# The last transform of a long convolution in eight 64x32 tiles, and the order of its gates, copies and stores

## The chip, the cores and the metric

The kernel runs on one core of one Trainium2 chip. Its engines work side by side, each on its own queue in order: TensorE (PE in the profile; PEld is its weight load), VectorE (DVE), ScalarE (ACT), GpSimd (POOL) and SyncE (SP), which here only issues DMAs. ACT and POOL can issue DMAs too. The metric is the device time of one execution in microseconds, as the median of several runs.

## The reference

A block in the manner of S4 with a gated feed-forward part, in float32, for L = 2048 positions and D = 512 channels:

```
xn = layernorm(x)
s  = causal_conv(xn, K) + xn * Dskip      # K from A, B, C, log_dt; done by FFTs of length 2L
g  = silu(gelu(xn @ w1 + b1) @ w2 + b2)
out = x + s * g
```

The convolution has one kernel of 2048 taps for each channel.

## The kernel before

A first long part (to about 400 us) makes the convolution kernels and the feed-forward part, whose gates g lie in DRAM in `gd`. The change does not touch it. The second part does the convolution for four blocks b of 128 channels. A transform over 2048 positions is split into N1 = 32 by N2 = 64, and for each block these steps run:

- `first_dft` (L873): matmuls over the 32, for the input and for the convolution kernel; ACT copies the result to SBUF (`X`, L879).
- `second_dft` (L892): matmuls over the 64, in 64x64 tiles. ACT copies the spectrum of the input (`uh`, L900), DVE multiplies it with that of the kernel (`product`, L909) and forms sums and differences (`combine`, L919 and L921, into `Y`).
- `back_dft` (L927, `sa`): the transform back over the 64; ACT copies into `Z` (L936).
- `swing` (L942, `w`): 128x128 transposes of `Z`, two for each of four row blocks q4; ACT, or DVE for some copies of the last block, copies to `bs` (L950).
- `last_dft` (L969, `y`): the transform back over the 32, with the cosine table `gc`. For one q4 it is two matmuls (jj = 0, 1) of 128 rows and 64 columns, 512 wide, into the two halves of one PSUM bank. Half of the table's entries are zeros: each of its 128 rows belongs to one of two interleaved halves hh of the output rows.
- `last_out`: DVE multiplies by the gate (L974, `gb`), POOL adds x (L975, `xb`); `store` (L981) writes the result, and `tail_load` (L959, L961) has fetched gate and x.

The order of the work is written out by hand. `slot(b, g)` for g = 0 to 7 does the second transforms of four of the 32 frequencies of block b, and beside them, in even slots, a quarter of the first transform of block b+1, in odd slots the back transform of a quarter that is done, and the last steps (swings, last transform, gate, store) of block b-1: in blocks 1 and 2 the swings stand in slots 3 and 5, two q4 each, and the last transforms in slots 5 and 7, two q4 each; in block 3 one q4 per slot, swings in slots 3 to 6 and last transforms in 4 to 7. Within a slot the instructions go out in the order second, first, back, copies, product, combine, last transform and gate and store, swings, loads. Block 3's own last steps run after its slot 7.

PSUM banks for all but the second transform come from `bank` (L821), in turn from two pools of two buffers. A matmul into a bank waits until the copy or the gate that read its last content is done. A tile of SBUF that is used again waits in the same way: the gate and x tiles of blocks 0 to 2 have three buffers each. All loads and stores of the last steps are issued by SP, in program order; for block 3 they go to a tile (`big`, called `last`) in a buffer that the transforms no longer need.

Of the kernel before, what the change touches and what calls it, by code (L numbers as in the profile page):

```python
# [125 lines left out]
def _shape_constants():  # L126
# [40 lines left out]
def kernel(  # L167
# [5 lines left out]
    V, A, GP, PE, SY = nc.vector, nc.scalar, nc.gpsimd, nc.tensor, nc.sync  # L173

    x_l = u[0].rearrange("(r j q) d -> j r q d", j=2, q=NQ)
    o_l = out[0].rearrange("(r j q) d -> j r q d", j=2, q=NQ)

# [627 lines left out]
    def open_mid():  # L805
        SB["pm"] = pm = opened(p2, "pm", "right")
        SB["ps"] = opened(pz, "psm", "left", bufs=2, space=PSUM)
        SB["tcn"] = pm.tile([P, N1, P], F32, name="tcn")
        SB["gc"] = pm.tile([P, 2 * N1], F32, name="gc")

# [118 lines left out]

    def back_out(b, j, h, eng=A):  # L930
        if (b, "Z") not in yy:
            yy[b, "Z"] = SB["pm"].tile([P, 4, 8, N1, 4], F32, tag="Z", name=f"Z{b}", bufs=2)
        k = 8 * j + 4 * h
        src = yy.pop((b, j, h)).rearrange("p k (x h) -> p x k h", h=4)
        dst = yy[b, "Z"].rearrange("p r q k h -> p (r q) k h")[:, :, k:k + 4, :]
        eng.copy(dst, src) if eng is A else eng.tensor_copy(dst, src)  # L936

    def swing(b, q4, jj):
        Z = yy[b, "Z"].rearrange("p (j r) (t q) k h -> p j r t q (k h)", j=2, t=2)
        p = bank(f"w{b}_{q4}_{jj}")  # L940
        for e in range(4):
            PE.transpose(p[:, e, :], Z[:, jj, q4 // 2, q4 % 2, e, :], ident)  # L942
        yy[b, q4, jj] = p

    def swing_out(b, q4, jj):
        if jj == 0:
            yy[b, q4, "s"] = SB["pm"].tile([P, 2, 4, P], F32, tag="bs", name=f"bs{b}_{q4}", bufs=3)
        dst = yy[b, q4, "s"][:, jj].rearrange("p e (x r) -> p e r x", r=2)
        src = yy.pop((b, q4, jj)).rearrange("p e (r x) -> p e r x", r=2)
        A.copy(dst, src) if jj or b < NB - 1 else V.tensor_copy(dst, src)  # L950

    gx = {}

    def tail_load(b, q4):
        cs = slice(b * P, (b + 1) * P)
        n = slice(4 * q4, 4 * q4 + 4)
        t = gx.pop((b, q4, "t"), None) or new_tail(b, q4)
        gx[b, q4] = t
        SY.dma_start(t[0], gd[b].rearrange("p (q m) -> p q m", m=P)[:, n])  # L959
        for j in range(2):  # L960
            SY.dma_start(t[1][j * 64:(j + 1) * 64], x_l[j, :, n, cs])  # L961

    def new_tail(b, q4):
        return tuple(SB["pm"].tile([P, 4, P], F32, tag=m, name=f"{m}{b}_{q4}", bufs=3) for m in ("gb", "xb"))

    def last_dft(b, q4):
        py = bank(f"y{b}_{q4}")
        for jj in range(2):
            PE.matmul(py[64 * jj:64 * jj + 64], SB["gc"], yy[b, q4, "s"][:, jj], start=True, stop=True, skip_group_check=True)  # L969
        gx[b, q4, "y"] = py  # L970

    def last_out(b, q4, eng):
        gb, xb = gx[b, q4]
        V.tensor_mul(gb, gx.pop((b, q4, "y")), gb)  # L974
        eng.tensor_add(xb, gb, xb)  # L975

    def store(b, q4):
        cs = slice(b * P, (b + 1) * P)
        xb = gx.pop((b, q4))[1]
        for j in range(2):  # L980
            SY.dma_start(o_l[j, :, 4 * q4:4 * q4 + 4, cs], xb[j * 64:(j + 1) * 64])  # L981

# [4 lines left out]

    def lasts(b, q4, eng=GP):
        last_dft(b, q4)
        last_out(b, q4, eng)  # L990

    def slot(b, g):
# [60 lines left out]
    with tc.manual_schedule():  # L1053
# [79 lines left out]
```

## Time and profile before

| | us |
|---|---|
| median of three runs | 598.95 |
| lowest, highest | 595.91, 600.62 |
| the profiled execution | 600.56 |
| its span, first to last instruction | 598.80 |

All times in the text are counted from the start of the span. PE is granted 0.98 of its full clock in the mean. The rows of the profile stand in the prediction. A row of a timeline is start, duration of the merged stretch, engine, line, operation, output <- inputs, shape, count, and in brackets the idle time ahead and what ended it. Each float32 matmul shows as two records. Durations of neighbouring matmuls overlap by the pipeline's depth; the distance from one start to the next tells what a group costs.

### The profile page before, as it was taken

Reading aid. Unit: us, or ns where it says so; the run is one execution under the profiler, and the core shown is the slowest. Engines: PE = TensorE matmul, PEld = TensorE weight load, DVE = VectorE, ACT = ScalarE, POOL = GpSimd, SP = SyncE. Lnnn points to the kernel's source line nnn. Section 1 sums busy time; section 2 is a strip of 40 time slices with the busy share of each in tenths; the row PEclk is TensorE's granted clock in tenths of the full one; section 3 lists DMA queues with packets and bytes.
Section 4 is the critical chain, followed back from the end, with each engine's and each line's share of the span. In section 5 each row is a group of like instructions: output and inputs, shape, how many; then the busy total and the mean of one; then the engine's idle time right before and its main releaser. Section 6 shows DMA issues by size and latency. Waiting matters only on the chain.

```text
span 598.8 us, 16788 instructions
## 1 busy us (share of the span) xinstructions
PE 551.5 (92%) x7064; PEld 440.8 (74%) x7064; DVE 466.2 (78%) x745; ACT 423.2 (71%) x613; POOL 267.8 (45%) x362
## 2 busy tenths in 40 slices
PE   1968999999959999999998999989999999999995
PEld 1656777777737777777776777767889887887872
DVE  5999998899999979999968898960047645765884
ACT  2567878699876999997999898853355555464442
POOL 1545646844577666597364656820220204202121
PEclk9989999999989999999999999989999999999998
DMA  8984522194717284205624338049846593613957
GB/s 189 322 232 132 198 63 91 40 297 134 252 54 281 86 272 146 99 22 175 178 75 165 92 119 104 23 124 297 225 151 75 148 104 71 177 40 74 186 123 152
DMA packets 100288, 86.62 MB, mean 145 GB/s; under 512 B 43538, under 2 KB 88850, under 8 KB 97140
## 3 DMA queue, kind: packets, MB, share of 16 engines
q1 hardware_dynamic: 97584, 67.71, 44.4%
q0 software_dynamic: 2624, 17.83, 8.3%
q8 instruction: 55, 0.90, 0.6%
q14 instruction: 21, 0.17, 0.1%
q10 hardware_dynamic: 4, 0.00, 0.0%
HBM read 51.97 MB, written 33.55 MB: 143 GB/s over the span
## 4 chain that ended last, share of the span: by engine, by line
PE 51%; DVE 7%; ACT 6%; DMA 3%; issue 2%; POOL 0%; DVEq 0%; ACTq 0%; POOLq 0%
PE s L892 10%; PE s L873 7%; PE sa L927 5%; PE f L245 4%; PE z L292 4%; PE f L246 4%; PE f L247 4%; PE z L293 3%; PE z L294 3%; PE kg L643 3%; PE w L942 2%; PE y L969 2%; DVE e L628 1%; PE ph L582 1%; DVE e L632 1%
## 5 line engine op out<-in xcount | busy, mean ns | idle before, releaser
L605 POOL TENSOR_TENSOR mm<-mm,rc 128x32 f32<-128x32 f32 (+4 forms) x150 | 104.7, 698 | 11.8
L292 PE MATMUL z<-w2h,hh 128*128 128x512 f32 x224 | 96.0, 429 | 0.2 <-ACT hh L270 0.2
L245 PE MATMUL f<-xh,w1h 128*128 128x512 f32 x220 | 93.4, 424 | 0.5 <-ACT hf L264 0.5
L294 PE MATMUL z<-w2h,hl 128*128 128x512 f32 x224 | 88.0, 393 | 0.4 <-DVE hl L280 0.4
L293 PE MATMUL z<-w2l,hh 128*128 128x512 f32 x224 | 87.7, 392 | 0.0
L246 PE MATMUL f<-xl,w1h 128*128 128x512 f32 x220 | 86.8, 395 | 0.0
L247 PE MATMUL f<-xh,w1l 128*128 128x512 f32 x220 | 86.3, 392 | 0.0
L909 DVE TENSOR_TENSOR t<-s,uh 128x512 f32<-128x512 f32 x64 | 41.2, 686 | 47.0 <-ACT uh L900 46.8
L280 DVE TENSOR_TENSOR hl<-hf,hh 128x512 fp32r<-128x512 f32 x56 | 42.4, 764 | 31.4 <-ACT hh L270 31.3
L892 PE MATMUL s<-X,mc 64*64 64x128 f32 x2048 | 63.1, 272 | 0.0
L892 PEld LDWEIGHTS s<-X,mc 64*64 64x64 f32 x2048 | 55.8, 133 | 5.1 <-issue 3.3
L602 POOL COPY mm<-rc 128x32 f32<-128x32 f32 x30 | 12.6, 420 | 102.8 <-DVE e L635 94.7
L628 DVE TENSOR_TENSOR e<-mm,ra 128x1024 f32<-128x1024 f32 x32 | 45.9, 1433 | 15.0 <-ACT ra L616 12.5
L879 ACT COPY X<-s 128x512 f32<-128x512 f32 x64 | 33.2, 598 | 32.6 <-PE s L873 32.6
L975 POOL TENSOR_TENSOR xb<-gb,xb 128x512 f32<-128x512 f32 x12 | 15.1, 1274 | 85.9 <-DVE gb L974 73.4
L245 PEld LDWEIGHTS f<-xh,w1h 128*128 128x128 f32 x220 | 42.4, 193 | 11.7 <-ACT hf L264 2.7
L294 PEld LDWEIGHTS z<-w2h,hl 128*128 128x128 f32 x224 | 42.2, 188 | 11.1 <-DVE hl L280 1.9
L264 ACT ACTIVATE hf<-f,b1s 128x512 f32<-128x512 f32 x56 | 38.2, 687 | 16.3 <-PE f L247 13.7
L292 PEld LDWEIGHTS z<-w2h,hh 128*128 128x128 f32 x224 | 42.5, 190 | 9.5 <-issue 0.7
L247 PEld LDWEIGHTS f<-xh,w1l 128*128 128x128 f32 x220 | 41.9, 190 | 9.1
L246 PEld LDWEIGHTS f<-xl,w1h 128*128 128x128 f32 x220 | 42.0, 191 | 8.1 <-DVE xl L380 0.2
L293 PEld LDWEIGHTS z<-w2l,hh 128*128 128x128 f32 x224 | 42.4, 189 | 7.4
(153 smaller groups left out, 1208.7 us busy)
## 6 DMA issues: line engine op xcount, KB each, us to landing
x<-in_A_u_dram SPq DMA_DIRECT2D x16, 256.0 KB
xs<-x SPq DMA_DIRECT2D x16, 256.0 KB
xt_h<-xh POOLq DMA_DIRECT2D x4, 1024.0 KB, 5.3
xt_l<-xl POOLq DMA_DIRECT2D x4, 1024.0 KB, 8.6
kgd<-ko SPq DMA_DIRECT2D x32, 128.0 KB
za<-zo SPq DMA_DIRECT2D x4, 1024.0 KB
xh<-xt_h POOLq DMA_DIRECT2D x4, 1024.0 KB, 5.8
xl<-xt_l POOLq DMA_DIRECT2D x4, 1024.0 KB, 7.9
```

Of the source, the lines that this page charges most:

```text
L245: PE.matmul(p, wh[:, k, :], xh[:, k, :], start=(k == 0), stop=False)
L246: PE.matmul(p, wh[:, k, :], xl[:, k, :], start=False, stop=False)
L247: PE.matmul(p, wl[:, k, :], xh[:, k, :], start=False, stop=(k == KD - 1))
L280: V.tensor_sub(hl, hf, hh)
L292: PE.matmul(z, hh[:, s], wh, start=(f0 == 0 and f > 0), stop=False)
L293: PE.matmul(z, hh[:, s], wl, start=False, stop=False)
L294: PE.matmul(z, hl[:, s], wh, start=False, stop=(f0 == FA - 1))
L605: GP.tensor_mul(mv[:, :, 0:3:2, w:2 * w], mv[:, :, 0:3:2, 0:w], rc[:, 2 + 2 * i:4 + 2 * i, :].rearrange("p j c -> p c j").unsqueeze(3).to_ ...
L628: V.tensor_mul(e1, m1.unsqueeze(1).to_broadcast([P, 2, CH, N1]), ra[:, :, :, :N1])
L873: PE.matmul(p[:, i, :], src[r, 2 * i:2 * i + 2, :], fc[r], start=True, stop=True, skip_group_check=True)
L892: PE.matmul(p[ka * 64:(ka + 1) * 64, r, o, :, jj], mc[h, k, ((0, 2), (1, 0))[c][o], :], xf[b][h, c, :, k, :], start=(c == 0), stop=(c == 1 ...
L909: V.tensor_mul(t, p[:, i, :, 1].unsqueeze(1).to_broadcast([P, 2, 2, P]), uh)
```

## The change

- The table `gc` loses its zeros: 128 rows by 32 columns, with the two halves hh above one another. `last_dft(b, t)` takes two q4 at once (t = 0, 1) and does eight matmuls of 64 rows by 32 columns, 512 wide, into two banks (h = 0, 1), four column groups each. `Z` is laid out anew so that the rows of one half stand together.
- A unit of gate, x and output is now (t, h). Its rows lie differently in DRAM, so that a load takes six DMAs (two for the gate, four for x) where it took three, and a store four where it took two.
- In the slots of blocks 1 and 2 the last transform, its gates and its stores go out straight behind the second transform of slots 5 and 7, ahead of the back transform, the copies and the products. In block 3 the last transform stands there too, in slots 4 and 7, with gates and stores behind the sums; its swings come one slot earlier, in slots 2 to 5.
- Block 2's units 2 and 3 get a buffer of their own (`spare`), and their loads come in slots 2 and 3. Block 3's own loads are issued by POOL in slots 1 to 4, instead of SP in slots 2, 3, 6 and 7.
- At the end, the last copy into Z is halved between ACT and DVE; the copies of q4 = 2 and 3 go to ACT alone; the last transforms come behind the third and the fourth swing; of each pair of gates POOL adds x to the first and DVE to the second; and stores go to SP, ACT and, for the last two, POOL.

```diff
-    cg = np.zeros((2, 2, N1, N1, 2))
-    for hh in range(2):
-        cg[hh, 0, :, :, hh] = np.cos(a).T
-        cg[hh, 1, :, :, hh] = -np.sin(a).T
-    cg = cg.transpose(2, 0, 1, 3, 4).reshape(P, 2 * N1)
+    cg = np.stack([np.cos(a).T, -np.sin(a).T], 1)
+    cg = np.stack([cg, cg]).reshape(P, N1)
...
-    def back_out(b, j, h, eng=A):
+    def back_out(b, j, h, engs=(A,)):
         if (b, "Z") not in yy:
-            yy[b, "Z"] = SB["pm"].tile([P, 4, 8, N1, 4], F32, tag="Z", name=f"Z{b}", bufs=2)
+            yy[b, "Z"] = SB["pm"].tile([P, 32, 2, N1, 2], F32, tag="Z", name=f"Z{b}", bufs=2)
...
-        A.copy(dst, src) if jj or b < NB - 1 else V.tensor_copy(dst, src)
+        A.copy(dst, src) if jj or b < NB - 1 or q4 > 1 else V.tensor_copy(dst, src)
...
+    def tail_load(b, i, q=SY):
...
+        for a in range(2):
+            r = slice(a * 64, (a + 1) * 64)
+            q.dma_start(t[0][r], gd[b].rearrange("(j n h) (t a q m) -> t h a j n q m", n=N1, h=2, t=2, a=2, m=P)[i // 2, i % 2, a])
+            for j in range(2):
+                r = slice(a * 64 + j * N1, a * 64 + (j + 1) * N1)
+                q.dma_start(t[1][r], x_t[i // 2, i % 2, a, j, :, :, cs])
...
-    def last_dft(b, q4):
-        py = bank(f"y{b}_{q4}")
-        for jj in range(2):
-            PE.matmul(py[64 * jj:64 * jj + 64], SB["gc"], yy[b, q4, "s"][:, jj], start=True, stop=True, skip_group_check=True)
-        gx[b, q4, "y"] = py
+    def last_dft(b, t):
+        py = [bank(f"y{b}_{t}_{h}") for h in range(2)]
+        for a in range(2):
+            for jj in range(2):
+                for h in range(2):
+                    r, m = slice(h * 64, (h + 1) * 64), N1 * (2 * a + jj)
+                    PE.matmul(py[h][m:m + N1], SB["gc"][r], yy[b, 2 * t + a, "s"][r, jj], start=True, stop=True, skip_group_check=True)
+        gx[b, t, "y"] = py
+
+    def last_out(b, t, engs):
+        py = gx.pop((b, t, "y"))
+        for h in range(2):
+            gb, xb = gx[b, 2 * t + h]
+            V.tensor_mul(gb, py[h], gb)
+            engs[h].tensor_add(xb, gb, xb)
+
+    def store(b, t, qs=((SY, SY), (SY, SY))):
+        cs = slice(b * P, (b + 1) * P)
+        for h in range(2):
+            xb = gx.pop((b, 2 * t + h))[1]
+            for a in range(2):
+                for j in range(2):
+                    r = slice(a * 64 + j * N1, a * 64 + (j + 1) * N1)
+                    qs[h][a].dma_start(o_t[t, h, a, j, :, :, cs], xb[r])
...
-        sw = {3: (0,), 4: (1,), 5: (2,), 6: (3,)} if last else {3: (0, 1), 5: (2, 3)}
-        ls = {4: (0,), 5: (1,), 6: (2,), 7: (3,)} if last else {5: (0, 1), 7: (2, 3)}
+        sw = {2: (0,), 3: (1,), 4: (2,), 5: (3,)} if last else {3: (0, 1), 5: (2, 3)}
+        ls = {4: (0,), 7: (1,)} if last else {5: (0,), 7: (1,)}
         second_dft(b, g)
+        if b:
+            for q4 in ls.get(g, ()):
+                last_dft(b - 1, q4)
+                if not last:
+                    last_out(b - 1, q4, (GP, GP))
+                    store(b - 1, q4)
...
-        if b:
-            for q4 in ls.get(g, ()):
-                lasts(b - 1, q4)
-                store(b - 1, q4)
+        if last:
+            for q4 in ls.get(g, ()):
+                last_out(b - 1, q4, (GP, GP))
+                store(b - 1, q4)
...
-        if b and g in (0, 1, 2, 5):
-            tail_load(b - 1, (0, 1, 2, 5).index(g))
-        if last and g in (2, 3, 6, 7):
-            tail_load(b, (2, 3, 6, 7).index(g))
+        if last and g == 2:
+            spare = SB["pf"].tile([P, 4, 4, P], F32, tag="in", name="spare", bufs=2)
+            for i in range(2):
+                gx[b - 1, 2 + i, "t"] = (spare[:, 2 * i], spare[:, 2 * i + 1])
+        when = (0, 1, 2, 3) if last else (0, 1, 2, 5)
+        if b and g in when:
+            tail_load(b - 1, when.index(g))
+        if last and 0 < g < 5:
+            tail_load(b, g - 1, GP)
...
-            back_out(b, 3, h)
-        for q4 in range(4):
+            back_out(b, 3, h, (A, V) if h else (A,))
+        for q4 in range(3):
             swings(b, q4)
-            if q4:
-                lasts(b, q4 - 1, V if q4 % 2 else GP)
-                store(b, q4 - 1)
-        lasts(b, 3, V)
-        store(b, 3)
+        last_dft(b, 0)
+        swings(b, 3)
+        last_out(b, 0, (GP, V))
+        store(b, 0, ((SY, SY), (A, A)))
+        last_dft(b, 1)
+        last_out(b, 1, (GP, V))
+        store(b, 1, ((SY, SY), (A, GP)))
```

More of the change, by code (lines that the diff above doesn't have):

```diff
@@ L173 @@
     V, A, GP, PE, SY = nc.vector, nc.scalar, nc.gpsimd, nc.tensor, nc.sync
+    x_t = u[0].rearrange("(n h j t a q) d -> t h a j n q d", n=N1, h=2, j=2, t=2, a=2)
+    o_t = out[0].rearrange("(n h j t a q) d -> t h a j n q d", n=N1, h=2, j=2, t=2, a=2)
     x_l = u[0].rearrange("(r j q) d -> j r q d", j=2, q=NQ)
-    o_l = out[0].rearrange("(r j q) d -> j r q d", j=2, q=NQ)
     dram = ctx.enter_context(tc.tile_pool(name="dram", bufs=1, space=DRAM))
@@ L808, in open_mid @@
         SB["tcn"] = pm.tile([P, N1, P], F32, name="tcn")
-        SB["gc"] = pm.tile([P, 2 * N1], F32, name="gc")
+        SB["gc"] = pm.tile([P, N1], F32, name="gc")
     def table_load(t, src):
@@ L928, in back_dft @@
         yy[b, j, h] = p
-    def back_out(b, j, h, eng=A):
+    def back_out(b, j, h, engs=(A,)):
         if (b, "Z") not in yy:
-            yy[b, "Z"] = SB["pm"].tile([P, 4, 8, N1, 4], F32, tag="Z", name=f"Z{b}", bufs=2)
+            yy[b, "Z"] = SB["pm"].tile([P, 32, 2, N1, 2], F32, tag="Z", name=f"Z{b}", bufs=2)
         k = 8 * j + 4 * h
-        src = yy.pop((b, j, h)).rearrange("p k (x h) -> p x k h", h=4)
-        dst = yy[b, "Z"].rearrange("p r q k h -> p (r q) k h")[:, :, k:k + 4, :]
-        eng.copy(dst, src) if eng is A else eng.tensor_copy(dst, src)
+        src = yy.pop((b, j, h)).rearrange("p k (x h c) -> p x h k c", h=2, c=2)
+        dst = yy[b, "Z"][:, :, :, k:k + 4, :]
+        w = 4 // len(engs)
+        for i, eng in enumerate(engs):
+            n = slice(w * i, w * i + w)
+            eng.copy(dst[:, :, :, n], src[:, :, :, n]) if eng is A else eng.tensor_copy(dst[:, :, :, n], src[:, :, :, n])
     def swing(b, q4, jj):
-        Z = yy[b, "Z"].rearrange("p (j r) (t q) k h -> p j r t q (k h)", j=2, t=2)
+        Z = yy[b, "Z"].rearrange("p (j r t q) h k c -> p j r t q (h k c)", j=2, r=2, t=2)
         p = bank(f"w{b}_{q4}_{jj}")
@@ L949, in swing_out @@
         src = yy.pop((b, q4, jj)).rearrange("p e (r x) -> p e r x", r=2)
-        A.copy(dst, src) if jj or b < NB - 1 else V.tensor_copy(dst, src)
+        A.copy(dst, src) if jj or b < NB - 1 or q4 > 1 else V.tensor_copy(dst, src)
     gx = {}
-    def tail_load(b, q4):
+    def tail_load(b, i, q=SY):
         cs = slice(b * P, (b + 1) * P)
[L956 to L961, printed above, removed]
+        t = gx.pop((b, i, "t"), None) or new_tail(b, i)
+        gx[b, i] = t
+        for a in range(2):
[4 more added lines that the diff above has]
+                q.dma_start(t[1][r], x_t[i // 2, i % 2, a, j, :, :, cs])
```

14 lines of the change are left out of this document (3 added, 11 removed).

## The prediction

> **What bounds the kernel now.** I read the page first (the engines' busy time, then the chain of work that ended last), then busy time by stretches, then the timelines of TensorE (PE), VectorE (DVE) and the DMA queues from 480 us on, where the diff acts.
>
> ```profile
> PE 551.5 (92%) x7064; PEld 440.8 (74%) x7064; DVE 466.2 (78%) x745; ACT 423.2 (71%) x613; POOL 267.8 (45%) x362
> PE 51%; DVE 7%; ACT 6%; DMA 3%; issue 2%; POOL 0%; DVEq 0%; ACTq 0%; POOLq 0%
> core 0: us, PE busy (x) PEld busy (x) DVE busy (x) ACT busy (x) POOL busy (x), PEclk, DMA share, GB/s
> 510.80:550.80 40.00, 39.14 (x882) 33.48 (x880) 23.90 (x37) 21.85 (x40) 5.38 (x6) 1.00 0.43 105
> 550.80:584.40 33.60, 32.93 (x642) 27.40 (x640) 26.94 (x44) 15.05 (x26) 7.38 (x6) 1.00 0.69 140
> 584.40:598.80 14.40, 7.90 (x48) 4.38 (x48) 7.37 (x11) 2.53 (x4) 1.50 (x2) 0.86 0.73 155
> ```
>
> PE is busy 92% and carries half of the chain. In block 2 (510.8 to 550.8 us) it is busy 39.1 of 40 us, and in block 3 (to 584.4) 32.9 of 33.6, with DVE at 26.9 there. So up to 584.4 what leaves PE's path is won as long as DVE keeps up, and block 3 is where DVE could fail to. After 584.4 the end is a ladder of short steps in which PE works only 7.9 of 14.4 us.
>
> The timeline of block 2's odd slots 5 (from 532.44) and 7 (from 545.07); columns are start, duration, engine, line, operands (s at L892 the second transform, s at L873 the first one, sa the back transform, w the transposes, y the last transform), and the wait ahead of it:
>
> ```profile
> 511.95 1.29 DVE L974 TENSOR_TENSOR gb<-y,gb 128x512 f32<-128x512 f32 x2
> 512.74 2.55 PE L873 MATMUL s<-fc,in 32*128 32x64 f32 x64
> ...
> 526.75 1.91 PE L942 MATMUL w<-ident,Z 128*128 128x128 f32 x16
> ...
> 530.50 2.01 PE L873 MATMUL s<-fc,in 32*128 32x64 f32 x64
> 532.44 1.98 PE L892 MATMUL s<-X,mc 64*64 64x128 f32 x64
> 534.35 2.05 PE L927 MATMUL sa<-tcn,Y 128*128 128x128 f32 x16
> 536.33 1.94 PE L969 MATMUL y<-bs,gc 128*64 128x512 f32 x8
> 538.20 1.09 PE L942 MATMUL w<-ident,Z 128*128 128x128 f32 x8
> 540.04 1.25 PE L942 MATMUL w<-ident,Z 128*128 128x128 f32 x8 [0.75 <-DVE gb L974]
> 541.22 1.98 PE L892 MATMUL s<-X,mc 64*64 64x128 f32 x64
> ...
> 545.07 1.98 PE L892 MATMUL s<-X,mc 64*64 64x128 f32 x64
> 546.98 2.05 PE L927 MATMUL sa<-tcn,Y 128*128 128x128 f32 x16
> 548.96 1.94 PE L969 MATMUL y<-bs,gc 128*64 128x512 f32 x8
> 550.83 3.72 PE L892 MATMUL s<-X,mc 64*64 64x128 f32 x128
> ```
>
> The reader is to see that starts follow one another with no gap but one: the second eight transposes of slot 5 wait for the gate (gb, L974), which frees the PSUM bank that they write.
>
> **The change, part by part.** First the tiles. Two row blocks' last transforms take 1.87 us (548.96 to 550.83), one alone 1.01 (rows below, 564.88 to 565.89): each is two tiles of 64 columns side by side, two passes long, so a third and a fourth pass add 0.86. Afterwards both row blocks are eight tiles in two passes. If all eight stream at once, the pair costs what one costs now, 1.01 plus the starts of six more tiles: I take 1.05. No row shows four column groups at once; the bounds are 1.01 and the 1.87 of today. Four pairs lie in the slots of blocks 1 and 2: 4 x 0.82 = **3.3 us** off PE's path.
>
> Second, the order in those slots. The last transform now comes ahead of sa, and its gates ahead of the products in DVE's queue. So the bank is free when w arrives, and the wait goes. The transposes in slot 5 take 3.02 us (538.20 to 541.22) and would take some 1.87 unbroken (the 1.91 of 526.75): 1.15 each in blocks 1 and 2, **2.3 us**. Behind it the next wait would be for ACT's copies of sa, a transpose earlier in the queue, which block 2's slot 3 (526.75) shows costs nothing. In block 2's slot 0 the first transform takes 2.55 instead of 2.01, because its banks were held by gates that run at 511.95, late; they now run early in slot 7: **0.5 us**. Together 6.1.
>
> ```profile
> 562.98 1.98 PE L892 MATMUL s<-X,mc 64*64 64x128 f32 x64
> 564.88 1.08 PE L969 MATMUL y<-bs,gc 128*64 128x512 f32 x4
> 565.89 1.09 PE L942 MATMUL w<-ident,Z 128*128 128x128 f32 x8
> ...
> 574.75 1.08 PE L969 MATMUL y<-bs,gc 128*64 128x512 f32 x4
> ...
> 578.68 2.05 PE L927 MATMUL sa<-tcn,Y 128*128 128x128 f32 x16
> 580.67 1.08 PE L969 MATMUL y<-bs,gc 128*64 128x512 f32 x4
> 581.67 2.05 PE L927 MATMUL sa<-tcn,Y 128*128 128x128 f32 x16
> 584.40 1.97 PE L942 MATMUL w<-ident,Z 128*128 128x128 f32 x16 [0.68 <-ACT Z L936]
> 581.68 0.87 DVE L919 TENSOR_TENSOR Y<-t,t 64x256 f32<-64x256 f32 x2
> 582.57 0.69 DVE L974 TENSOR_TENSOR gb<-y,gb 128x512 f32<-128x512 f32 x1
> ```
>
> Third, block 3. Up to the end of slot 6's second transform (574.75, that is 23.92 us behind the block's start at 550.83) PE now does two y and three w; afterwards one y of 1.05 and four w, because all transposes come a slot earlier: 23.92 - 2.02 + 1.05 + 1.02 = 23.97. So nothing is won there. But slots 6 and 7 are then two bare second transforms in a row, and DVE sets the pace. From the end of slot 7's second transform (578.68) to the end of DVE's sums (581.68 + 0.87 = 582.55) there are 3.87 us today; afterwards slot 6's chain takes that from 23.97, and slot 7's product and sums queue behind it: two products of 0.686 (row below) and four half sums of 0.43, 3.1 us. The sums end at 23.97 + 3.87 + 3.1 = 30.94, against 31.72 today. PE has by then done slot 7's second transform, y and sa (some 6 us), so the last back transform starts from the sums, as now; from there to the first transposes lie 1.85 us (582.55 to 584.40), in which DVE's half of the last copy fits, though two gates of 0.69 are ahead of it. Gain 0.8.
>
> ```profile
> L909 DVE TENSOR_TENSOR t<-s,uh x64: 680/686/694, 443.3 to 580.1; 128x512 f32<-128x512 f32 x64
> L634 DVE TENSOR_TENSOR e<-mm,ra x32: 674/685/2546, 70.7 to 396.9; 128x512 f32<-128x512 f32 x32
> L975 POOL TENSOR_TENSOR xb<-gb,xb x12: 1267/1274/1282, 500.1 to 583.3; 128x512 f32<-128x512 f32 x12
> L961 SPq DMA_DIRECT2D xb<-in_A_u_dram x24: 595/625/2018, 470.9 to 578.5; - x24
> L981 SPq DMA_DIRECT2D out_dram<-last x8: 595/619/631, 588.9 to 595.0; - x8
> 588.90 6.68 SPq L981 DMA_DIRECT2D out_dram<-last  x8
> 590.51 0.64 ACT L950 COPY bs<-w 128x512 f32<-128x512 f32 x1 [1.38 <-PE w L942]
> 443.10 3.07 POOL L433 DMA_DIRECT2D gd<-zi  x4 [10.47 <-ACT zi L431]
> gd<-zi POOLq DMA_DIRECT2D x4, 256.0 KB, 3.5
> ```
>
> Fourth, what the early gates put behind them: products, then sums, then sa. In most slots sa comes two slots later and nothing is felt. In block 2's slot 7 it is not so: block 3 has no first transforms, and sa starts 1.05 + 1.98 + 3.7 (y, sa, two second transforms) = 6.7 us after that second transform, while DVE needs 1.25 (y and its signal) + 1.38 (gates) + 1.35 (products) + 2.8 (sums) = 6.8. There is no cover left, and two things can add to it. One is SP's queue: DMAs per row block double (six loads, and four stores for each half), each about 0.65 us from start to start, so between slot 5's gate and slot 7's second gate SP issues eight stores and four of six loads; counted from the end of slot 5's y, gate and POOL's addition (2.2) + 12 x 0.65 = 10.0 plus a landing, with the gate due at 11.6. [...] The other is POOL: its two additions of 1.27 us start with the gates and now reach into DVE's sums. L634, with both inputs in SBUF as the sums have, takes 0.685 in the median but up to 2.55 where POOL works beside it; L909, with one input in PSUM, never goes over 0.694. [...] I take **1.0 us** lost here, nearer to the low end because both parts can also be nil, between 0 and 3.8 (1.9 and 2.55 - 0.69). Block 3 in all: 0.2 lost.
>
> Block 3's own loads go to POOL's queue: eighteen issues at the 0.77 of gd<-zi (3.07 us for four) are 14 us, begun about 2 us into the block, before additions due at 18: hidden by 2 us, and POOL is not needed sooner. Stores and loads of block 2 on SP (32 issues, 21 us from about 5) also end before anything waits for them.
>
> Fifth, the end, counted from the first transposes. Before, SP's last store is issued by 595.58 (588.90 + 6.68), 11.2 us behind 584.40. Now six groups of transposes run through (2.65), y of the first half (to 3.8), the last two groups (to 4.8). All but two copies out go to ACT, so that the last pair (0.64 each, from 4.6 on) ends at 5.9, and the second y at 6.9 with its last pass and its signal; gate 7.8, POOL's addition 9.1, four stores on SP 11.8: 0.6 later than now. [...] I take **0.8 us** lost, between 0 and 1.6.
>
> Sum: -6.1 + 0.2 + 0.8 = -5.1 us. The profiled execution took 600.56 us (span 598.80), 1.6 above the median of the three runs, 598.95; the same difference gives 593.9. The smaller cosine table, and the copies into Z (same element count on ACT, other strides), I cost at nothing: ACT is busy 15.1 of 33.6 us in block 3.
>
> **The rivals.** *Four column groups share what two have.* Then y stays at 1.87: +3.3 in the slots, +0.8 in block 3, +1.2 at the end, which gives 599.2. For it: no row shows more than two column groups of this width. Against: two of 64 columns lose nothing (1.01 for both). Chance 0.12.
>
> *Slower: the column groups stream one after another.* Place: y. Four groups of two passes of 0.43 are 3.5 us, 2.45 more than forecast, in about 7.5 of the eight places (half of slot 7's hides behind DVE): +18, about 612. It decides from a y of 1.7 us on (nothing won), and is 1% slower from 2.5. Against it stands the same pair of 64-column tiles. Chance 0.13.
>
> [...] Chance 0.13.
>
> **How the numbers follow.** My forecast, 593.9, has 0.62. Its unknown terms (y 1.01 to 1.87 belongs to the rival; block 2's slot 7 0 to 3.8; the end 0 to 1.6) reach from 592.1 to 597.5, and the three runs lie 4.7 apart, so that their median may be off by 1.5: 591 to 599. The range reaches up to the first rival, 591.0 to 600.0, and leaves out the slower rival and a little below. About 1%, 6 us, can be told from no change. 1% faster is below 592.96, which is 0.9 under the forecast: of its 0.62, 0.32 falls there and 0.30 not, and 0.01 comes from the third rival. Slower by 1%: 0.12 of the second rival and 0.01 of the first. Faster 0.33, within 0.54, slower 0.13.
>
> **What would show it.** Eight-tile groups of y spanning 1.0 to 1.1 us start to start; no wait of w for gb in slot 5; slots 5 and 7 of block 2 of 6.8 and 4.95 us; PE waiting for DVE's Y by about 1 us at block 3's first sa, and again at its last one; from the first w of the end to the end of the span 15.0 to 15.5 instead of 14.4. A y of 1.87 or 3.5 makes the prediction wrong at its first step, a gate waiting for a load in slot 7 by over 2 us at its fourth.

## The result, and the profile after

The changed kernel takes 596.62 us (median of 20 runs, 594.09 to 600.09), the kernel before 600.14 on the same chip (20 runs, 595.91 to 602.14). The ratio is 0.9951, with a 95% interval of 0.9935 to 0.9967: half a per cent faster, and the interval leaves out 1. The forecast was 593.9; the time lies in its range of 591 to 600. Measured against the median before, the forecast's 5.1 us became 2.9 to 3.5. (Another 1.2 us of the miss come from the base: the three runs that the forecast started from had a median of 598.95.)

The profiled execution took 600.09 us, the longest of the 20, with a span of 598.3. Busy time by stretches (blocks 2 and 3 and the end, columns as in the prediction):

```profile
core 0: us, PE busy (x) PEld busy (x) DVE busy (x) ACT busy (x) POOL busy (x), PEclk, DMA share, GB/s
507.10:545.60 38.50, 36.91 (x897) 32.77 (x897) 24.42 (x36) 21.67 (x40) 5.92 (x7) 1.00 0.43 109
545.60:581.18 35.58, 31.91 (x657) 27.27 (x656) 29.35 (x48) 15.26 (x27) 18.17 (x29) 1.00 0.67 154
581.18:598.30 17.12, 8.44 (x64) 5.75 (x64) 6.49 (x8) 3.54 (x6) 5.01 (x6) 0.71 0.42 93
```

Block 2 is 1.5 us shorter than before (40.00), block 3 is 2.0 us longer (33.60) although PE works 1.0 us less in it, and the end is 2.7 us longer (14.40), with a granted clock of 0.71 in the mean instead of 0.86. From block 1's slot 5 to block 3's start the profile gains 4.5 us, and behind that it gives all of it back.

PE's timeline in the slots:

```profile
510.95 1.96 PE L890 MATMUL s<-X,mc 64*64 64x128 f32 x60
514.50 0.43 PE L890 MATMUL s<-X,mc 64*64 64x128 f32 x4 [1.59 <-issue]
...
530.19 1.98 PE L890 MATMUL s<-X,mc 64*64 64x128 f32 x64
532.09 1.09 PE L975 MATMUL y<-bs,gc 64*32 64x512 f32 x16
533.11 2.05 PE L925 MATMUL sa<-tcn,Y 128*128 128x128 f32 x16
535.00 1.91 PE L943 MATMUL w<-ident,Z 128*128 128x128 f32 x16
536.84 1.98 PE L890 MATMUL s<-X,mc 64*64 64x128 f32 x64
```

The eight tiles of a pair of row blocks take 1.02 us (532.09 to 533.11), as one took before, and no gate stands ahead of w any more: this slot is 6.65 us long instead of 8.78. The five places on which the forecast counted give 6.5 us (it said 6.1): slots 5 and 7 of blocks 1 and 2 give 2.1, 0.85, 2.1 and 0.85, slot 0 of block 2 0.5. But in block 2's slot 1 PE stops for 1.6 us, four records before the end of a second transform, for nothing that the profile shows; in the kernel before it stopped once too, in block 1's slot 2, and lost 0.8. The changed profile has a second stop in block 3's slot 5 (0.44 us, 566.38 to 566.82), by which that slot's second transform takes 2.71 us instead of 1.91; the control below has none there.

DVE's two gates of slot 7 and PE's rows at the seam of blocks 2 and 3, then the SP queue of the slots before:

```profile
543.84 0.69 DVE L982 TENSOR_TENSOR gb<-y,gb 128x512 f32<-128x512 f32 x1 [3.00 <-issue]
546.67 0.69 DVE L982 TENSOR_TENSOR gb<-y,gb 128x512 f32<-128x512 f32 x1 [2.14 <-DMA gb<-gd]
...
548.70 1.98 PE L890 MATMUL s<-X,mc 64*64 64x128 f32 x64 [1.13 <-DVE t L907]
...
551.45 1.83 PE L925 MATMUL sa<-tcn,Y 128*128 128x128 f32 x14 [0.17 <-DVE Y L917]
```

```profile
535.41 5.21 SPq L992 DMA_DIRECT2D out_dram<-xb  x8
540.72 0.45 SPq L961 DMA_DIRECT2D gb<-gd  x1
541.28 2.14 SPq L964 DMA_DIRECT2D xb<-in_A_u_dram  x2
543.47 0.45 SPq L961 DMA_DIRECT2D gb<-gd  x1
```

Slot 7's second gate could run at 544.5 and runs at 546.67, 3.2 us behind the issue of its second half load, which stands in SP's queue behind slot 5's eight stores and three more loads. Products, sums and PE queue behind it: the first back transform of block 3 gets going 5.85 us behind the block's start (545.60 to 551.45) instead of 3.65. This is the delay of the forecast's fourth step: 2.2 us here, not 1.0. (Two of the back transform's records had run before the wait; at the second transform behind it, 553.21, the delay is 2.0.)

The end, and the last pieces of the chain of work that ended last (start, us, what):

```profile
578.97 1.30 PE L925 MATMUL sa<-tcn,Y 128*128 128x128 f32 x8 [0.89 <-DVE Y L917]
...
581.18 4.51 PE L943 MATMUL w<-ident,Z 128*128 128x128 f32 x24 [0.92 <-DVE Z L937]
...
590.98 1.26 DVE L983 TENSOR_TENSOR last<-last 128x512 f32<-128x512 f32 x1
592.54 1.09 POOL L992 DMA_DIRECT2D out_dram<-last  x2 [0.84 <-DVE last L983]
```

```profile
592.54 0.55 POOL out_dram L992
593.09 0.54 POOLq L1154
```

Two things are new here. The 24 transposes take 4.51 us, where 16 took 1.97 before: the granted clock is 0.5 from 581.69 to 585.10. And the chain ends with POOL's two stores. They have landed by about 595.7 (the second issued at 593.09, 2.6 us from issue to landing), SP is done at 596.2, but POOL's closing drain, the instruction behind its stores at L1154, runs from 592.99 to 597.53 (4.54 us) and holds the end.

### The profile page after: what moved, and what is told of

Same layout as the page of the kernel before. It is cut to its first block, busy times and chain, and to the rows that moved or that the text cites. A ratio compares the mean times of both kernels' runs of the same rounds, so it can differ in the third digit from the quotient of the medians.

```text
span 598.3 us, 17036 instructions
## 1 busy us (share of the span) xinstructions
PE 546.1 (91%) x7128; PEld 440.6 (74%) x7128; DVE 466.3 (78%) x743; ACT 423.3 (71%) x615; POOL 283.2 (47%) x389
## 4 chain that ended last, share of the span: by engine, by line
PE 45%; DVE 31%; ACT 12%; issue 6%; POOL 2%; DMA 1%; SPq 1%; POOLq 0%; DVEq 0%; ACTq 0%
PE s L890 8%; PE s L871 7%; PE sa L925 4%; DVE e L626 4%; PE f L243 3%; PE z L290 3%; PE f L244 3%; PE f L245 3%; DVE e L630 3%; PE z L291 3%; PE z L292 3%; PE kg L641 3%; PE w L943 3%; DVE hl L278 3%; DVE ra L594 2%
## 5 line engine op out<-in xcount | busy, mean ns | idle before, releaser
L626 DVE TENSOR_TENSOR e<-mm,ra 128x1024 f32<-128x1024 f32 x32 | 46.0, 1438 | 15.1 <-ACT ra L614 15.0
L630 DVE TENSOR_TENSOR e<-mm,ra 128x1024 f32<-128x1024 f32 x32 | 45.9, 1435 | 0.0
```

Of the source, the lines that this page charges most:

```text
L626: V.tensor_mul(e1, m1.unsqueeze(1).to_broadcast([P, 2, CH, N1]), ra[:, :, :, :N1])
L630: V.tensor_mul(e2[:, :, :, :H], m2[:, :, :H].unsqueeze(1).to_broadcast([P, 2, CH, H]), ra[:, :, :, dn])
```

## The experiments

Each kernel was timed beside the kernel before on the same chip: kernels 1 to 4 on one, the control and 5 to 7 on a second, 8 to 11 on a third. The control, 3, 4 and 5 have 12 runs, the other numbered kernels 6. The stages below are from one profiled execution each, start to start: A is from the start of block 1's slot 5 to block 3's start, B from there to the first transposes of the end, C from those to the end of the span.

| kernel | median us | ratio to before, 95% | A | B | C |
|---|---|---|---|---|---|
| before | 600.14 | | 58.60 | 33.57 | 14.40 |
| changed | 596.62 | 0.9951 (0.9935-0.9967) | 54.11 | 35.58 | 17.12 |
| changed, again (control) | 596.80 | 0.9952 (0.9932-0.9971) | 54.05 | 34.41 | 15.49 |
| 1 gate loads earlier | 593.84 | 0.9892 (0.9843-0.9941) | 53.61 | 33.24 | 17.15 |
| 2 no stores from POOL | 594.76 | 0.9896 (0.9850-0.9942) | 53.34 | 34.62 | 14.14 |
| 3 filling transposes | 596.42 | 0.9925 (0.9894-0.9955) | 53.80 | 34.53 | 15.63 |
| 4 old order in blocks 1, 2 | 603.38 | 1.0046 (1.0014-1.0078) | 57.79 | 35.15 | 17.12 |
| 5 tiles computed twice | 599.39 | 0.9986 (0.9965-1.0007) | 56.62 | 34.49 | 15.44 |
| 6 edits 1, 2 and 3 | 593.81 | 0.9899 (0.9871-0.9927) | 52.98 | 33.54 | 14.10 |
| 7 = 6, swings in slots 3 to 6 | 593.46 | 0.9893 (0.9867-0.9919) | 53.46 | 33.12 | 14.31 |
| 8 = 7, later kernel loads | 591.95 | 0.9884 (0.9846-0.9921) | 52.62 | 33.20 | 14.04 |
| 9 = 7, last copy whole | 593.44 | 0.9901 (0.9867-0.9936) | 53.06 | 33.05 | 14.11 |
| 10 = 8 and 9 | 591.67 | 0.9887 (0.9848-0.9926) | 52.89 | 32.85 | 14.06 |
| 11 = 10, one fill | 591.71 | 0.9878 (0.9850-0.9906) | 53.14 | 33.41 | 14.24 |

The intervals are 2 to 6 us wide from end to end, so neighbours in this table are told apart by their stages, not by their medians; a stage is one execution, which has its own stops of PE (last section).

**The control: the changed kernel again.**

> The changed kernel again, unedited, as the measure for the other kernels of this group. Theory (the half clock at the end depends on how TensorE's two waits fall into stretches of 3.41 us, so it comes in some executions only): from the first transposes of the end to the end of the span it is 15.5 to 15.8 us where the clock stays full there and 17.0 to 17.2 where it halves. Rival (the clock halves in every execution): 17.0 to 17.2 again. The median lies 1.5 to 4.5 us under the kernel before on the same chip.

C is 15.49 with the clock full and 17.12 with it halved for 3.41 us, so the half clock comes in some executions and costs some 1.6 us where it comes. B is 1.2 shorter than in the first profile: 0.4 at block 3's first back transform, 0.8 the stop in slot 5. The stop in block 2's slot 1 is the same in both profiles of this kernel (1.59 us).

**1. The gate's load earlier.** `gb` gets a fourth buffer, and unit 3's gate rows are fetched in slot 3:

```
-            tail_load(b - 1, when.index(g))
+            tail_load(b - 1, when.index(g), parts="gx" if last or g < 5 else "x")
+        if b and not last and g == 3:
+            tail_load(b - 1, 3, parts="g")
```

> Blocks 1 and 2: the gates' tiles get a fourth buffer, and the gate rows of unit 3 are loaded in slot 3 instead of behind slot 5's stores (its x rows stay in slot 5). Theory (the late load cost what the forecast put at 1.0 and the trace shows as 2.2 us): the second gate of slot 7 in block 2 waits under 0.2 us for its load, the first back transform of block 3 starts 3.8 to 4.8 us behind the block's start instead of 5.85, and the time is 1.2 to 2.2 us under the changed kernel's. [...]

```profile
541.25 1.29 DVE L983 TENSOR_TENSOR gb<-y,gb 128x512 f32<-128x512 f32 x2 [3.00 <-issue]
542.07 2.52 POOL L984 TENSOR_TENSOR xb<-gb,xb 128x512 f32<-128x512 f32 x2 [8.03 <-issue]
543.77 2.07 DVE L919 TENSOR_TENSOR Y<-t,t 64x512 f32<-64x512 f32 x2
...
547.31 1.83 PE L925 MATMUL sa<-tcn,Y 128*128 128x128 f32 x14 [0.16 <-DVE Y L917]
```

Its timeline shows both gates of slot 7 in one piece, and the back transform in full 4.30 us behind the block's start (543.01). In the four profiles of the changed kernel's load it is 5.85, 5.47, 5.40 and 5.60 (changed, control, 2 and 3), so the load costs 1.1 to 1.55 us, and another 0.65 are left over the 3.65 of the kernel before. Those 0.65 are POOL's: with the gates on time its two additions (542.07 to 544.59) reach into the sums, of which the first two take 2.07 us, where they take 1.39 in the changed kernel (548.59). Both are in it; the load is the larger. (The ratio says 3.6 us under the control; its interval is wide, and the stages do not show more than the load.)

**2. The last stores without POOL.**

```
-        store(b, 1, ((SY, SY), (A, GP)))
+        store(b, 1, ((SY, SY), (A, A)))
```

> The last two stores are issued by ScalarE instead of GpSimd. Theory (GpSimd's closing drain, 592.99 to 597.53 us in the profile of the changed kernel, ends 1.35 us behind SyncE's at 596.20 and sets the end): the end becomes SyncE's, and the time falls by 1.0 to 1.4 us. Rival (the drain is an effect of that one execution, or ScalarE's two further issues and their landing end as late): under 0.4 us.

```profile
576.16:590.30 14.14, 6.78 (x64) 4.08 (x64) 6.49 (x8) 3.47 (x6) 3.93 (x4) 0.92 0.53 113
```

C is 14.14 (its row by stretches, above). The control's row for the same stretch:

```profile
580.41:595.90 15.49, 6.77 (x64) 4.08 (x64) 6.49 (x8) 3.45 (x6) 5.01 (x6) 0.80 0.47 103
```

PE, DVE and ACT do the same work in both. Among the executions with the clock full up to the last transposes, those whose last stores leave through POOL have 15.49, 15.63 and 15.44 (control, 3, 5), those without 14.04 to 14.31 (2 and 6 to 11): POOL costs 1.1 to 1.6 us, whatever else is changed. Without it, the new end is as short as the old one. POOL no longer holds the end: the chain that ended last has no piece of POOL on kernel 2's page, where the changed kernel's ends with POOL's stores and what stands behind them (592.54 and 593.09). (The ratio says 3.4 us under the control, more than the 1.0 to 1.4 expected; its interval is wide, and C shows 1.35.)

**3. No idle TensorE ahead of the last transposes.**

```
+        idle = SB["ps"].tile([P, 8, P], F32, tag="ri", name="idle", bufs=2)
+        for e in range(7):
+            PE.transpose(idle[:, e, :], ident, ident)
         for h in range(2):
             back_dft(b, 3, h)
             back_out(b, 3, h, (A, V) if h else (A,))
+        for e in range(7):
+            PE.transpose(idle[:, e, :], ident, ident)
```

> Seven transposes of the identity, which nobody reads, stand ahead of the last back transform and seven more behind it, so that TensorE does not idle for 0.89 and 0.92 us there. Theory (two waits in one stretch of 3.4 us halve the granted clock for the next 3.4 us, in which the 24 transposes take 4.51 us instead of some 2.7): the clock stays full until 590 us at least, the transposes take 2.6 to 2.9 us, and the time falls by 1.3 to 1.8 us. Rival (the clock fell for another reason, or the copies pace the transposes): the transposes keep 4 us or more, and the time changes by less than 0.5 us.

The clock stays full until TensorE is done, at 583.9 us (the expectation said 590; the page has it at 0.8 of full in the last slice, 577.9 to 592.7), and the transposes take 2.84 us. But they take 2.84 in 2, 5 and the control too, which have no fill, and the ratio, 1.6 us under the control's, has an interval that overlaps with it. So the gain in the time is not shown. When the clock halves is read from PE's busy time in the stretch of 3.41 us ahead of the place where it could. One row each of the changed kernel and of kernel 5, by stretches:

```profile
578.28:581.69 3.41, 1.80 (x13) 1.55 (x14) 2.66 (x6) 0.80 (x2) 1.61 (x2) 1.00 0.00 0
```

```profile
578.18:581.60 3.42, 1.87 (x14) 1.43 (x12) 3.19 (x7) 1.22 (x3) 0.85 (x1) 1.00 0.02 5
```

After 1.80 us of work in 3.41 the next stretch runs at half clock, after 1.87 it does not. The two others that halve (1 and 4) have 1.73 and 1.62, and the control 2.53 and 2.50, because there the two waits of 0.9 us fall into different stretches. The stretches lie on a grid that does not start with the kernel: the changed kernel's clock changes at 581.69, 585.10 and 591.93, whole multiples of 3.41 apart. So of the six executions without fill three halve, and of the seven with one fill or two (3 and 6 to 11) none does. The stretches ahead of the three were not idle: PE was busy for 1.62 to 1.80 of their 3.41 us.

PE's busy time alone does not decide it, though. Kernel 8, behind its last transposes:

```profile
580.33:583.74 3.41, 1.41 (x16) 0.22 (x14) 3.11 (x4) 0.31 (x1) 1.82 (x2) 1.00 0.51 115
583.74:587.15 3.41, 0.00 (x0) 0.00 (x0) 0.61 (x1) 0.00 (x0) 0.06 (x1) 1.00 0.83 189
```

Behind 1.41 us of work the clock stays full, and so it does in kernel 4 behind 1.82 (496.26 to 499.67); in the changed kernel it halves behind 2.25 (397.39 to 400.78), there for 6.82 us. So 1.80 against 1.87 is no general threshold; what is counted was not found.

**4. The tiles in the old order.** In blocks 1 and 2 the last transform, gates and stores stand behind the sums again:

```
-                last_dft(b - 1, q4)
-                if not last:
-                    last_out(b - 1, q4, (GP, GP))
-                    store(b - 1, q4)
+                if last:
+                    last_dft(b - 1, q4)
...
-        if last:
+        if b:
             for q4 in ls.get(g, ()):
+                if not last:
+                    last_dft(b - 1, q4)
                 last_out(b - 1, q4, (GP, GP))
```

> In blocks 1 and 2 the last transform, its gates and its stores go back behind the sums, as in the kernel before; the eight tiles, block 3 and the end stay. Theory (tiles 3.3 us, order 2.8 us, late load 2.2 us): the transposes of slot 5 wait for the gate again, 0.7 to 1.2 us in blocks 1 and 2, block 3's first back transform starts 3.7 to 4.3 us behind the block's start, and the time is 0 to 1.2 us above the changed kernel's. Rival 1 (the order is worth nothing beside the tiles): 1.5 to 2.2 us below it. Rival 2 (no late load in most executions, the order worth its 2.8): 2.3 to 3 us above it.

```profile
499.34 1.25 PE L943 MATMUL w<-ident,Z 128*128 128x128 f32 x8 [1.59 <-DVE gb L982]
...
512.00 0.43 PE L871 MATMUL s<-fc,in 32*128 32x64 f32 x2 [0.38 <-DVE gb L982]
512.60 1.99 PE L871 MATMUL s<-fc,in 32*128 32x64 f32 x58 [0.17 <-DVE gb L982]
...
571.95 1.16 PE L925 MATMUL sa<-tcn,Y 128*128 128x128 f32 x8 [2.07 <-DVE gb L982]
```

None of the three times held, though block 3's first back transform starts 3.66 us behind the block's start, as expected: by the ratios it is 5.6 us (0.94%) over the control, and slower than the kernel before. (The spans of the two profiles differ by 5.9 us, of which 1.6 are the half clock that comes in this one and not in the control's.) The tiles make y 0.85 us shorter, and in slot 5 the wait for the gate grows by as much, from 0.75 to 1.59, because the gate's time is set by DVE's queue of products and sums and not by y. Slot 5 of block 1 is 8.78 us long, and was 8.99. In slot 7 the 0.85 is won and lost again one slot later, where the first transform waits for the gates' banks (slot 0 of block 2 5.24 instead of 4.39). And in block 3 a gate waits 3.7 us for a DMA, since the loads stand behind stores that now come late, and takes 2.07 of PE's time with it. Tiles alone save 0.8 us in A (1.1 in the five places). So the forecast's 3.3 for the tiles is there only with the new order.

**5. The order with the old price of y.** In blocks 1 and 2 all tiles are computed twice:

```
-        for a in range(2):
+        for a in (0, 1) * (2 if b < 2 else 1):
```

> In blocks 1 and 2 the eight tiles of the last transform are computed twice over, so that a pair costs 2.04 us of TensorE again, with the new order kept. Theory (with the gates ahead of the products TensorE sets the pace there, and the late load hides what is added in block 2's slot 7): the other three pairs cost 1.0 us each, 2.6 to 3.4 us over the changed kernel, and the transposes of slot 5 still wait for no gate. Rival 1 (VectorE or ScalarE paces those slots): under 1.5 us. Rival 2 (slot 7 pays too): 3.8 to 4.3 us.

```profile
532.15 1.95 PE L975 MATMUL y<-bs,gc 64*32 64x512 f32 x32
534.03 2.05 PE L925 MATMUL sa<-tcn,Y 128*128 128x128 f32 x16
535.91 1.91 PE L943 MATMUL w<-ident,Z 128*128 128x128 f32 x16
```

A pair takes 1.88 us again (532.15 to 534.03), and no gate stands ahead of w. All four pairs cost 0.86 more in A, 3.4 together; of slot 7's share in block 2 half comes back, since block 3's first back transform then gets going 4.99 us behind the block's start instead of the control's 5.47. That leaves 3.0; the medians differ by 2.6, the ratios by 2.0, with wide intervals. In the new order PE sets the pace: what y costs is what the kernel costs. And the order needs no cheaper y: in the five places this kernel is 3.3 us shorter than the kernel before (7.51 twice, 5.77 twice and 3.85), where the forecast gave the order 2.8. The order alone gives 3.3, the tiles alone 1.1, both together 6.5.

**6. The three repairs together.**

> The earlier gate load, the last stores from ScalarE and the filling transposes together. Theory (1.0 to 1.6 us of late load, 1.5 of GpSimd's drain, and half clock in a third of the executions at 1.5 us): 2.8 to 3.8 us under the changed kernel, 5.5 to 7 us under the kernel before; block 3's start to the first transposes of the end 33.0 to 33.5 us, from there to the end 14.0 to 14.4. Rival (they share what they save): within 2 us of the changed kernel.

```profile
506.99:544.56 37.57, 36.91 (x897) 32.77 (x897) 25.24 (x37) 21.69 (x40) 5.71 (x7) 1.00 0.45 115
544.56:578.10 33.54, 33.08 (x671) 28.69 (x670) 28.85 (x47) 15.29 (x27) 18.23 (x29) 1.00 0.71 159
578.10:592.20 14.10, 6.78 (x64) 4.08 (x64) 6.49 (x8) 3.45 (x6) 3.94 (x4) 0.91 0.53 113
```

3.0 us under the control, 6.1 (1.01%) under the kernel before by the ratio: B is back at 33.5 and C at 14.1, as expected, and the gain of the slots stays. By their ratios, edits 1 and 2 give nearly as much each (0.9892, 0.9896 against 0.9899), so only the stages divide the gain.

**7. Block 3's swings where they were**, on top of 6:

```
-        sw = {2: (0,), 3: (1,), 4: (2,), 5: (3,)} if last else {3: (0, 1), 5: (2, 3)}
-        ls = {4: (0,), 7: (1,)} if last else {5: (0,), 7: (1,)}
+        sw = {3: (0,), 4: (1,), 5: (2,), 6: (3,)} if last else {3: (0, 1), 5: (2, 3)}
+        ls = {5: (0,), 7: (1,)} if last else {5: (0,), 7: (1,)}
```

> As the kernel with the three edits together, but block 3's transposes of block 2 stand in slots 3 to 6 again, as in the kernel before, and the first pair of last transforms in slot 5 instead of 4. By the forecast's own step (the end of slot 6's second transform starts VectorE's closing chain of 6.97 us, and the transposes moved ahead of it cost 1.02 us): that end comes 1.0 us earlier, and so do the sums and the whole, 0.8 to 1.2 us under the kernel with the three edits. Rival (VectorE is behind before that and paces slots 6 and 7 whatever TensorE does first): within 0.3 us of it, with VectorE busy without a gap from slot 5 on.

The sums end 30.6 us behind block 3's start instead of 31.6 in kernel 6: the step holds. Only 0.4 of it reaches the transposes, and the whole is not 0.8 to 1.2 us faster as expected (0.35 in the medians, within the noise). DVE is not behind (it idles 0.8 us ahead of slot 6's product), so the rival falls; kernel 11 shows what takes the rest.

**8. Later loads of block 3's convolution kernel**, on top of 7:

```
-            kernel_load(b + 2)
+            if b + 2 < NB - 1:
+                kernel_load(b + 2)
...
+        if b == NB - 2 and g == 1:
+            kernel_load(NB - 1)
```

> As the kernel with block 3's swings in slots 3 to 6, but the two loads of 512 KB that fetch block 3's convolution kernel come in block 2's slot 1 instead of block 1's slot 6, with the skip term in slot 3. It tests TensorE's stop in block 2's slot 1 (0.66 to 1.59 us in the profiles with the new slots, ending 1.3 to 1.5 us behind a 16 KB load of the instruction queue). Theory (the instruction load comes late because it stands behind those 1 MB in the DMA engines): no stop above 0.3 us there, and no other of that size in blocks 1 to 3. Rival (the instructions are asked for late, whatever else moves): a stop of 0.6 us or more in slot 1, within a few matmuls of the same place.

```profile
525.63 0.65 PE L890 MATMUL s<-X,mc 64*64 64x128 f32 x10
526.57 1.75 PE L890 MATMUL s<-X,mc 64*64 64x128 f32 x54 [0.29 <-issue]
```

PE's stop in block 2's slot 1, 0.73 us in kernel 7, is gone, and one of 0.29 stands in slot 5; with the same loads it is 0.57 in kernel 10 and 0.81 in kernel 11. So PE stopped elsewhere when those loads came later, against the rival, but the stop moved more than it vanished, against the theory.

**9. The last copy into Z whole, by ScalarE**, on top of 7:

```
-            back_out(b, 3, h, (A, V) if h else (A,))
+            back_out(b, 3, h)
```

> As the kernel with block 3's swings in slots 3 to 6, but the last copy into Z is done whole by ScalarE, as in the kernel before. [...]

The last copy in kernel 7, and in this one:

```profile
576.80 0.37 ACT L937 COPY Z<-sa 128x256 f32<-128x256 f32 x1 [0.31 <-PE sa L925]
577.21 0.43 DVE L937 COPY Z<-sa 128x256 f32<-128x256 f32 x1 [0.73 <-ACT Z L937]
```

```profile
575.95 0.58 ACT L937 COPY Z<-sa 128x512 f32<-128x512 f32 x1 [0.31 <-PE sa L925]
```

The halves run one behind the other, DVE idle for 0.73 us until ACT's is done, where the whole takes 0.58 us: from the start of the last back transform to the first transposes it is 2.63 us without the split and 2.87 with it. The split costs 0.24 us; why DVE's half waits for ACT's was not tried.

**10. Edits 8 and 9 together.**

> Both of these edits together, as a candidate: later loads of block 3's convolution kernel and the whole copy on ScalarE, with the earlier gate load, the last stores from ScalarE, the filling transposes and the swings in slots 3 to 6. Theory: the gains of the two add to the 1.07 per cent under the kernel before that the base showed, 0.5 to 1.0 us more, 592.5 to 593.3 us. Rival (neither of the two matters): 593.3 to 594.0 us, the same as the base.

591.67 us, lower than either expectation, 1.1% under the kernel before; B has 9's share in it (32.85), the rest can't be told from 8.

**11. As 10, without the first fill.**

```
-        for e in range(7):
-            PE.transpose(idle[:, e, :], ident, ident)
         for h in range(2):
             back_dft(b, 3, h)
```

> As the candidate with both edits, without the first seven filling transposes (the seven behind the last back transform stay). It tests why the swings in slots 3 to 6 brought 0.4 us where the step promised 1.0, though the sums ended 1.05 us earlier. Theory (with the sums that early the first fill stands in the way: it delays the first half of the last back transform from 571.35 to 572.12 in the candidate's times, and with it the second half, whose sums end at 572.47): from block 3's start to the first transposes 32.2 to 32.5 us instead of 32.85. Rival (the copies into Z or ScalarE pace that place): 32.8 to 32.9. In the timed runs 0.5 us cannot be told apart; the trace decides.

```profile
558.65 2.25 PE L976 MATMUL y<-bs,gc 64*32 64x512 f32 x16
560.83 2.05 PE L925 MATMUL sa<-tcn,Y 128*128 128x128 f32 x16
...
568.98 1.09 PE L976 MATMUL y<-bs,gc 64*32 64x512 f32 x16
570.00 3.99 PE L925 MATMUL sa<-tcn,Y 128*128 128x128 f32 x32
573.82 0.93 PE L1129 MATMUL idle<-ident 128*128 128x128 f32 x7
574.66 2.84 PE L943 MATMUL w<-ident,Z 128*128 128x128 f32 x24
```

B as a whole is 33.41, because a last transform in slot 5 took 2.18 us instead of 1.02 (558.65 to 560.83): PE stops in the middle of it. Behind that the theory holds: from slot 7's y to the transposes it is 5.68 us (568.98 to 574.66), and 6.30 in kernel 10 (568.44 to 574.74). The fill had cost 0.6 us where the sums came early. Kernels 10 and 11 are faster than both the changed kernel and the one before, by 0.6 to 0.7% and by 1.1 to 1.2% in their ratios.

## Why the prediction was right in the slots and wrong behind them

Of the forecast's 5.1 us 2.9 came, by the ratio. What failed is not the tiles or the order but what follows them: the fifth step, the end, had the wrong thing at the end of its chain; the fourth, the early gates, was sized at half of what it cost; and PE's stops were put at nothing. The time, 596.62, is also that of the third rival (the forecast with the full 3.8 us lost in block 2's slot 7, 593.9 + 2.8 = 596.7), but by chance: that cost came only in part, and others made up the rest.

*The tiles* cost what was forecast: eight stream at once, 1.02 us for a pair; both rivals on column groups fall with that row. That this is worth 3.3 us by itself was wrong in the reasoning: kernel 4 wins 0.8 with it in A, since in the old order DVE's gate ends the waits and comes no earlier for a shorter y.

*The order* did what was said: no wait of w for a gate, slot 0's banks free in time. Tiles and order together gave 6.5 us of the 6.1 forecast, and kernel 5 shows that PE then sets the pace.

*Block 3.* In the control the sums end 0.8 us earlier, as forecast, counted from the second transform behind the first back transform (25.28 us instead of 26.08): the 6.97 us of DVE's chain behind slot 6's second transform were 6.95, and the 1.85 us from the sums to the transposes 1.91. The loads through POOL are over before its additions are due, as forecast. That the transposes moved a slot ahead cost 1.02 at the start of that chain was in the sum, and kernel 7 gets it back at the sums.

*The early gates* (step four) were mis-sized: 1.75 to 2.2 us in the four profiles that show them instead of the 1.0 taken, within the bounds of 0 to 3.8. Of it 1.1 to 1.55 is the load. By the forecast's own sign, a gate that waits over 2 us for its load in slot 7, the step is wrong in the changed kernel's profile (2.14) and just not in the three others (1.70 to 1.90). I took the cost nearer to the low end "because both parts can also be nil"; neither was. The load's part of the upper bound, 1.9, is 10.0 plus the 3.5 of gd<-zi less 11.6; that it can be nil rested on a quicker landing, which no run shows for this load. The landing was 3.2, and of the issues ahead of it the eight stores took the 0.65 us each that were reckoned, but two loads of x 2.14 together (541.28). The other part is POOL. DVE's rows of block 2's slots 5 and 7 in the changed kernel:

```profile
535.85 2.03 DVE L919 TENSOR_TENSOR Y<-t,t 64x512 f32<-64x512 f32 x2
...
548.59 1.39 DVE L919 TENSOR_TENSOR Y<-t,t 64x512 f32<-64x512 f32 x2
```

The sums beside POOL's additions (534.10 to 536.63) are stretched from 1.39 to 2.03 us, but in slot 5, where PE has other work; in slot 7 the late gate has moved POOL's addition ahead of the sums, and they take 1.39. It costs 0.64 and not a whole addition of 1.27; of the second addition 0.78 us are left when the sums start (535.85 to 536.63). So in the changed kernel the late load hides POOL's part. In kernel 1, where the gate is on time, slot 7's sums take 2.07, and these 0.68 us are what is left of the delay there. The two parts share their time instead of adding up to the 3.8 of the upper bound.

*The end* (step five) was the step that failed most. 0.8 us was taken, of which SP's stores are 0.6. The rest counted on DVE's addition standing still until POOL's is done, and on the landing of POOL's stores; the first no run shows: in the changed kernel DVE's addition starts 0.55 us behind POOL's (590.98 and 590.43) and takes 1.26 us, of which 0.71 are beside it, where in the kernel before it takes 0.69 with no addition of POOL beside it. POOL's last stores with the drain behind them cost 1.1 to 1.6, so that the control's end is 1.1 us longer than the old one, and the half clock, which the forecast has no term for, adds 1.6 in three of the six profiled executions without fill. The landing of POOL's stores of 64 KB, 2.6 us, is under the 3.5 of gd<-zi's 256 KB; it was not the landing that held the end.

*What had no term:* PE's stop in block 2, 2.0 us in the changed kernel and the control against 0.8 elsewhere in the one before. Whether the change brings it or only moves the place was not shown.

The sum for the control: slots -6.5, stop +1.2, block 3 +0.8 (forecast +0.2), end +1.1 (forecast +0.8), together -3.4; with the half clock in half of the executions, as in the profiles, -2.6. Measured: -2.9 by the ratio, -3.5 in the medians. The third rival was in part true, at its place and with some half of its price (1.75 to 2.2 of 3.8 us).

## What to carry to other kernels

A shorter matmul group pays only where the wait behind it is not set by another engine's queue (in kernel 4 a y shorter by 0.85 us brought a wait for DVE's gate longer by 0.84): look at what the next instruction waits for, and move the consumer first. When a step's DMAs double, count the queue up to the load that the earliest consumer needs, and give that load a buffer of its own (1.1 to 1.55 us here). At the end of a kernel like this one, keep DMAs off GpSimd (1.1 to 1.6 us here), and look for two short waits of TensorE within 3.4 us, since here two of 0.9 us went with a halved clock for the steps that followed.

## What was not expected of the hardware

GpSimd's closing drain lasts 4.54 us in the changed kernel, with its own stores just ahead, and 3.04 us in the kernel before, without. In the changed kernel it ends some 1.9 us after the stores have landed (597.53, and about 595.7). What it waits for was not tried.

TensorE's clock halved for 3.41 us after stretches of 3.41 us that were not idle: 1.62, 1.73 and 1.80 us of work ahead of the last transposes, and 2.25 at 397.39 us in the changed kernel, there for 6.82 us. It stayed full behind 1.87 at the same place in kernel 5, and behind 1.41 in kernel 8.

TensorE stops, for nothing that the profile names, once or twice in the last 130 us of every profiled execution here: 0.3 to 1.6 us in the middle of a row of matmuls, and 1.9 us ahead of one in kernels 4 and 7 (block 1's slot 1). The three stops in the profiles of the changed kernel and the kernel before (1.59, 0.44 and 0.57 us) each end 1.34 to 1.38 us after a 16 KB load in the queue that the profile's page calls "instruction": the loads end at 513.16, 565.46 and 480.76, the stops at 514.50, 566.82 and 482.14. In kernel 5, with 32 more records of TensorE ahead of it, the stop in block 2's slot 1 sits 32 records earlier, at record 28 instead of 60: it kept its place in TensorE's row of instructions. With other times for two data loads (kernel 8) the stop there, 0.73 us in kernel 7, is gone and one of 0.29 stands in slot 5. Why TensorE stops at such a place was not settled.
